# A transformer block on one core: loads held behind the modulation weights, gb folded into w_down, and a recut tail

## The chip, the cores and the metric

The kernel runs on one core of a Trainium2 chip. A core has five engines that run their own instruction streams and meet at semaphores: PE multiplies matrices, ACT applies functions, DVE does element-wise work, POOL a little of the same, and SP issues transfers (ACT can issue them too). The metric is the device time of one execution in microseconds. The time before is 896.17 us, the median of 3 runs (896.01 to 898.0). The changed kernel's time is compared with it.

## The reference

One block of a diffusion transformer: 2048 tokens, width 512, 32 heads of 16, and a gated FFN of width 1792, all bf16. A vector c gives six vectors of modulation.

```python
mod = (silu(c) @ w_mod).reshape(1, 6, 1, -1)         # w_mod 512 x 3072
sa, ca, ga, sb, cb, gb = ...                         # the six rows
h = layernorm(x) * (1 + ca) + sa
x = x + ga * attention(h)                            # 32 heads, then @ wo
h = layernorm(x) * (1 + cb) + sb
x = x + gb * ((gelu(h @ w_gate) * (h @ w_up)) @ w_down)
```

## The kernel before, in words

The kernel is written as a recorder. Each call (`mm`, `act`, `ts`, `tt`, `dma`) records one instruction for one engine, finds out which earlier instructions it must wait for from the bytes it touches, and adds the waits. Each engine then runs its list in the order in which it was recorded. So the order in the Python is the order on the engine, and a wait at one instruction holds everything behind it on that engine. SP's list is the queue of nearly all transfers.

There are three stages.

*The prologue* (`prologue`) is written out by hand. It loads c, the first four tiles of x (128 tokens each), the first third of `w_mod` (sa and ca, 1 MB) and the first 128 columns of Wq, Wk and Wv, then the rest of x, of Wqkv and of `w_mod`. PE runs filler matmuls (`warm_up`) meanwhile. silu(c) is computed by a Tanh; `mod_cols` turns it into eight columns of modulation; `ln_stat`, `ln_rstd` and `ln_norm` normalize the tiles; PE transposes them and `modulate` writes the first 512 tokens of `hT`, channels by tokens, in four channel blocks. K and Q of the first eight heads follow. `ln_rstd` runs on POOL: an addition of epsilon and a power of -0.5.

*The stream* (`stream`) is ordered by a planner that keeps its own clock of every engine while it records. Its backbone is the attention: for a group of 128 keys by 512 queries PE makes scores (`qk`), ACT takes the exponential of two or three such groups at a time (one 128 x 1024 or 128 x 1536 instruction over two or three PSUM banks), and PE multiplies by V (`pv_mms`). The planner gives some groups to DVE instead (`exp_load`, `exp_vec`: a polynomial in seven instructions over two groups). Everything else is side work in one ordered list (`plan`): the other projections, the modulation vectors, Wo, layer norm 2 and the FFN of one set of tokens after another; it is fitted in where PE has room, and its DVE steps are tasks (`task`, `step`). `SETS` cuts the queries into seven sets of 512, 512, 256, 256, 256, 128 and 128. A unit is one set with four heads (`qd` 0 to 7). `QS` says for how many `qd` the last two sets share a unit. The softmax sums go through DRAM (`pv_done`) for all units but the last ones, which use a matmul with `self32` (`near_end`, `tail_den`). The FFN inside the stream makes gelu from ACT's Tanh and DVE multiplications; `down_fin` multiplies the result by gb, adds x and stores the tile.

*The tail* (`tail`) runs when the last scores are recorded. The last set (`kb`) still needs its last sums, Wo, layer norm 2 and the whole FFN; the set before it (`ka`) has had `EARLY` chunks of its FFN's four in the stream and finishes here. `tail_end` and `tail_ffn` are generators from which the loop takes the matmul that it thinks ready first. Here gelu is an ACT function, whose table is loaded once.

In the profile nearly all instructions have the line of a helper: L308 is `mm`, L312 `transpose`, L321 `act`, L325 `tt`, L333 `ts`, L338 `stt`, L342 `copy`, L345 `recip`, L349 `memset`, L361 and L364 the statistics, L371 `dma`, L565 and L566 `ln_rstd`. They are told apart by tile: `ps_sc` is the six score banks, `ps_pv` and `ps_mi` one bank each, `E` the exponentials, `dreg` holds w_down (and, early, the normalized rows and the fillers' zeros), `mreg` w_mod and later w_gate and w_up, `wreg` Wqkv and later the FFN's input and gelu, `hreg` hT and later the FFN's product, `dt` and `dx` DVE's exponentials.

Of the kernel before, what the change touches and what calls it, by code (L numbers as in the profile page):

```python
# [14 lines left out]
P = 128  # L15
# [22 lines left out]
QS = 5  # L38
# [9 lines left out]
EARLY = 2  # L48
# [3 lines left out]
SOON = 100  # L52
END = (0, None)
# [26 lines left out]
class _Recorder:  # L80
# [285 lines left out]
    def dma(self, eng, out, in_, sem, noncontig=False, late=0):  # L366
        def fn(e):
            if noncontig:
                with self.nc.allow_non_contiguous_dma(reason="small strided transfer"):
                    return e.dma_start(out, in_)  # L370
            return e.dma_start(out, in_)  # L371
        n = mybir.dt.size(out.dtype)
        for _, k in out.ap:
            n *= int(k)
        op = self.rec(eng, fn, [in_], [out], dma=sem, cost=n)
        if op is not None:
            op.t1 += late
        return op
# [37 lines left out]
class _Kernel(_Recorder):  # L416
# [12 lines left out]
    def alloc(self):  # L429
# [32 lines left out]
        self.xw = hreg[:, NFC * 512:NFC * 512 + D]  # L462
# [7 lines left out]
        self.crow = dreg[:, 9 * D:10 * D]  # L470
        self.tcol = sb("tcol", [P, NDC], FP32)
# [17 lines left out]
    def prologue(self):  # L489
# [18 lines left out]
        self.memset(dve, self.warm, 0.0)  # L508
        self.memset(dve, self.ones[:, :], 1.0)
# [14 lines left out]
        for dc in range(NDC):  # L524
            self.mm(self.scp[:, 0, dc:dc + 1], self.crow[0:1, P * dc:P * dc + P], self.ones[0:1, 0:1])
        self.warm_up(16)
        self.act(self.tcol[:, :], self.scp[:, 0, 0:NDC], ACT.Tanh, scale=0.5)
# [3 lines left out]
        self.stt(self.tcol[:, :], self.tcol[:, :], 1.0, self.scp[:, 0, 0:NDC], ALU.add, ALU.mult)  # L531
        self.ts(dve, self.sc_bf[:, :], self.tcol[:, :], 0.5, None, ALU.mult)
# [29 lines left out]
    def ln_rstd(self, a, b):  # L562
        r = self.rstd[:, a:b]
        v, h = self.mv[:, a:b, 1], self.half[:, 0:b - a]
        self.rec("pool", lambda e: e.tensor_scalar(r, v, EPS, None, op0=ALU.add), [v], [r], cost=self.cost("pool", r, [v], "small"))  # L565
        self.rec("pool", lambda e: e.tensor_tensor(r, r, h, ALU.pow), [r, h], [r], cost=self.cost("pool", r, [r], "pow"))  # L566
# [18 lines left out]
    def mod_cols(self, bank, base):  # L585
        for ci in range(8):
            for dc in range(NDC):
                self.mm(bank[:, ci:ci + 1], self.wmod[:, dc, base + P * ci:base + P * ci + P],
                        self.sc_bf[:, dc:dc + 1], start=(dc == 0), stop=(dc == NDC - 1))
# [151 lines left out]
    def weight_parts(self):  # L741
# [11 lines left out]
        parts.append(part(self.wd[:, 12:NFC, :], v[:, 12:NFC, :], "wd12"))  # L753
# [8 lines left out]
    def scale_wo(self):  # L762
# [4 lines left out]
        yield from self.until("wo")  # L767

# [57 lines left out]
    def side_ffn(self, gi, part=None):  # L826
# [61 lines left out]
        if part is not None:  # L888
# [3 lines left out]
            return  # L892
        for i in range(n):
# [53 lines left out]
    def plan(self, ends, nsplit):  # L947
# [12 lines left out]
        w.append((lambda: self.side_q_all(2), at(133), at(160)))  # L960
        w.append((lambda: self.side_q_all(3), at(160), a + 40))
# [59 lines left out]
    def stream(self):  # L1021
# [72 lines left out]
        while pos < nseq:  # L1094
# [19 lines left out]
            if tq is not None and tq <= t + 30:  # L1114
# [9 lines left out]
                if (('v', 3, 0) in self.have and len(active) < NACT and sum(v >= 4 * rp for v in vec) < NED - (pend is None)  # L1124
                        and self.backlog() < BACK and self.free["dve"] < t + 700
                        and len(mem) == CH and slack > -100 and self.credit < (2600 if pos < ends[-3] else 1600)):
# [203 lines left out]
    def tail(self, ka, kb, half, rest):  # L1330
# [3 lines left out]
        gens += [self.tail_end(kb, f, l), self.tail_ffn(ka, self.pv[:, :], l, 0, ("part", ka))]  # L1334
        nxt = [None] * len(gens)
        table = False
        while True:
# [7 lines left out]
            best = None  # L1345
            for i, g in enumerate(gens):
# [6 lines left out]
                elif nxt[i] is not None:  # L1353
                    x = self.probe(nxt[i])
                    if best is None or max(x, t + 30) < best[0]:
                        best = max(x, t + 30), i
            w = self.next_side()
            if w is not None:
                x = self.probe(w[4][1])
# [132 lines left out]
```

## Time and profile before

| | |
|---|---|
| median of 3 runs | 896.17 us (896.01 to 898.0) |
| the profiled execution | 895.93 us, its span 894.2 us |
| ACT busy | 865.8 us, 97% of the span; of it 841.7 in exponentials |
| DVE busy | 816.4 us, 91% |
| PE busy | 811.3 us, 91% (a modelled figure) |
| granted TensorE clock | 1.00 throughout |
| modulation weights landed | 8.58 us |
| first exponential starts | 14.57 us |
| end of the last exponential | 872.55 us |
| PE's last matmul ends | 890.8 us |

A row of the timeline or of the chain gives start and length in us; a row of the groups gives the line, engine, operation, output and inputs with their shapes, the count, then busy time in us and the mean of one in ns, then the idle time of the engine ahead of it and who ended it.

### The profile page before, as it was taken

To read this page: it belongs to the slowest core of one execution; us is meant where nothing else is said; L and a number is where in the kernel's file an instruction comes from. 1 tells how busy PE (TensorE), PEld (TensorE's weight loads), DVE (VectorE), ACT (ScalarE), POOL (GpSimd) and SP (SyncE) were. 2 spreads that over 40 slices of the span, in tenths; PEclk is the share of its full clock that TensorE was granted. 3 is DMA by queue.
4 is the path that set the end of the run, shared out by engine and by line. 5 is a ranking of instruction groups with operands and counts; after the bars stand their busy time and mean duration, and the time that the engine had idled before them with its cause. 6 is when DMAs were issued, how large, how long until landed. Compare 5 with 4: busy or idle time off the path is not lost.

```text
span 894.2 us, 19936 instructions
## 1 busy us (share of the span) xinstructions
PE 811.3 (91%) x8661; PEld 286.7 (32%) x8661; DVE 816.4 (91%) x1500; ACT 865.8 (97%) x736; POOL 19.2 (2%) x36
## 2 busy tenths in 40 slices
PE   8899999988898898989999898999999999998998
PEld 3333222222222222222233222333333343334455
DVE  7778999999998999999998999998999999979955
ACT  4999999999999999999999999999999999999992
POOL 2100000000000000000000000000000000000000
PEclk9999999999999999999999999999999999999999
DMA  9012122000200000000000000010000000000100
GB/s 305 2 25 70 41 78 60 25 14 14 55 14 8 7 13 14 14 8 19 19 26 14 9 14 9 14 31 19 10 14 21 14 14 8 27 14 9 27 9 12
DMA packets 32509, 25.10 MB, mean 28 GB/s; under 512 B 16233, under 2 KB 28262, under 8 KB 32422
## 3 DMA queue, kind: packets, MB, share of 16 engines
q1 hardware_dynamic: 30566, 22.79, 8.6%
q8 instruction: 67, 1.10, 0.5%
q10 hardware_dynamic: 1856, 1.05, 0.4%
q14 instruction: 20, 0.16, 0.1%
HBM read 21.23 MB, written 2.61 MB: 27 GB/s over the span
## 4 chain that ended last, share of the span: by engine, by line
ACT 91%; PE 6%; DVE 2%; DMA 1%; issue 0%; SPq 0%
ACT E L321 88%; PE ps_sc L308 3%; ACT wreg L321 3%; PE ps_mi L308 2%; PE ps_pv L308 1%; DMA mreg<-in_w_mod_dram 1%; DVE st L361 0%; ACT hreg L321 0%; DVE dt L333 0%; DVE kmo L333 0%; DVE mreg L325 0%; DVE mreg L338 0%; SPq L371 0%; DVE hreg L325 0%; DVE wreg L338 0%
## 5 line engine op out<-in xcount | busy, mean ns | idle before, releaser
L321 ACT ACTIVATE E<-ps_sc 128x1536 bf16<-128x1536 f32 (+2 forms) x698 | 841.7, 1411 | 9.9 <-PE ps_sc L308 9.6
L308 PE MATMUL ps_sc<-qT,kme 32*128 32x256 bf16 (+2 forms) x1600 | 171.0, 304 | 13.8 <-ACT E L321 10.4
L308 PE MATMUL ps_sc<-qT,kmo 32*128 32x256 bf16 (+2 forms) x1664 | 172.2, 298 | 11.1 <-ACT E L321 7.9
L308 PE MATMUL ps_pv<-E,vaug 128*17 128x256 bf16 (+2 forms) x2884 | 179.8, 300 | 2.3 <-DVE osb L342 1.3
L333 DVE TENSOR_SCALAR dt<-ps_sc 128x512 int32<-128x512 f32 x204 | 139.0, 686 | 11.3 <-PE ps_sc L308 8.2
L308 PE MATMUL ps_sc<-kme,ident 128*128 128x512 bf16 x327 | 104.4, 384 | 36.9 <-ACT E L321 33.4
L308 PE MATMUL ps_mi<-wreg,mreg 128*128 128x256 bf16 (+2 forms) x624 | 123.6, 309 | 8.2 <-DVE wreg L342 4.0
L308 PEld LDWEIGHTS ps_sc<-qT,kmo 32*128 32x128 bf16 x1664 | 50.3, 92 | 120.2 <-ACT E L321 72.3
L308 PEld LDWEIGHTS ps_sc<-qT,kme 32*128 32x128 bf16 x1600 | 48.6, 92 | 125.2 <-ACT E L321 74.7
L308 PEld LDWEIGHTS ps_pv<-E,vaug 128*17 128x17 bf16 x2884 | 53.5, 88 | 96.8 <-issue 83.8
L325 DVE TENSOR_TENSOR qT<-qT,dx 128x1024 f16<-128x1024 f16 (+1 forms) x106 | 70.3, 664 | 1.3
L333 DVE TENSOR_SCALAR dx<-dt 128x1024 f16<-128x1024 uint16 (+1 forms) x107 | 70.0, 654 | 0.1
L308 PEld LDWEIGHTS ps_mi<-wreg,mreg 128*128 128x128 bf16 x624 | 47.7, 97 | 63.1 <-issue 30.1
L308 PE MATMUL ps_mi<-dreg,hreg 128*128 128x512 bf16 x210 | 65.3, 385 | 1.5 <-DVE wreg L338 0.8
L338 DVE SCALAR_TENSOR_TENSOR qT<-dt,qT 128x1024 int16<-128x1024 int32 (+1 forms) x53 | 62.3, 1176 | 0.1
L308 PEld LDWEIGHTS ps_sc<-kme,ident 128*128 128x128 bf16 x327 | 23.4, 97 | 88.1 <-ACT E L321 83.4
L325 DVE TENSOR_TENSOR ed<-ed,dx 128x1024 f16<-128x1024 f16 (+1 forms) x72 | 47.7, 662 | 0.7
L342 DVE CAST wreg<-ps_mi 128x512 bf16<-128x512 f32 x51 | 35.0, 686 | 11.3 <-PE ps_mi L308 10.8
L338 DVE SCALAR_TENSOR_TENSOR ed<-dt,ed 128x1024 int16<-128x1024 int32 (+1 forms) x36 | 42.2, 1172 | 0.2
L308 PE MATMUL ps_mi<-hreg,wreg 128*128 128x512 bf16 x120 | 38.7, 385 | 0.8 <-DVE vaug L342 0.5
L338 DVE SCALAR_TENSOR_TENSOR wreg<-wreg,ps_mi 128x512 bf16<-128x512 bf16 x51 | 34.7, 680 | 2.4 <-ACT wreg L321 1.8
L308 PE MATMUL ps_pv<-qT,vaug 128*17 128x256 bf16 (+2 forms) x178 | 36.5, 290 | 0.0
(126 smaller groups left out, 712.9 us busy)
## 6 DMA issues: line engine op xcount, KB each, us to landing
rb<-scr_rec SPq DMA_DIRECT2D x16, 256.0 KB
rb<-scr_rec SPq DMA_DIRECT2D x29, 128.0 KB
mreg<-in_w_mod_dram SPq DMA_DIRECT2D x1, 2048.0 KB, 12.9
out_dram<-xs SPq DMA_DIRECT2D x16, 128.0 KB, 1.7
mreg<-in_B_w_gate_dram SPq DMA_DIRECT2D x4, 448.0 KB, 7.2
mreg<-in_B_w_up_dram SPq DMA_DIRECT2D x4, 448.0 KB, 6.7
dreg<-in_B_w_down_dram SPq DMA_DIRECT2D x3, 512.0 KB, 7.6
wreg<-in_A_wqkv_dram SPq DMA_DIRECT2D x3, 384.0 KB, 9.8
```

What stands on the lines that cost most here:

```text
L308: return self.rec("pe", lambda e: e.matmul(out, lhsT, rhs, start=start, stop=stop, tile_position=tp), [lhsT, rhs], [out], cost=(n, int(rhs ...
L321: return self.rec("act", lambda e: e.activation(out, in_, func, scale=scale, **kw), rd, wr, cost=self.cost("act", out, [in_], "act" if bia ...
L325: return self.rec(eng, lambda e: e.tensor_tensor(out, a, b, op), [a, b], [out], cost=self.cost(eng, out, [a, b], "tt"))
L333: return self.rec(eng, lambda e: e.tensor_scalar(out, a, s1, s2, **kw), rd, [out], cost=self.cost(eng, out, [a], "ts" if len(rd) == 1 else ...
L338: return self.rec("dve", lambda e: e.scalar_tensor_tensor(out, a, s, b, op0=op0, op1=op1), rd, [out], cost=self.cost("dve", out, [a, b], " ...
L342: return self.rec(eng, lambda e: e.tensor_copy(out, in_), [in_], [out], cost=self.cost(eng, out, [in_], "ts"))
```

## The change

The prologue: ACT issues the first part of `w_mod` as its second transfer. The first columns of Wk, Wq and Wv are issued by SP with a dependence on that part (`after`), so SP waits for it, and all of SP's later transfers stand behind: the rest of x, which ACT's queue issued in part before, the rest of Wqkv and of `w_mod`. silu's factor of one half is folded into the matmuls that turn c (a column of 0.5 in place of ones), which saves a DVE instruction; the 1 + scale is added by PE (four matmuls of the identity with ones); two of sixteen fillers go. The modulation vector is copied by ACT. The transposes run tile by tile and not block by block, the last block's last two tiles into a bank of their own, so that ACT and DVE each take half of that block. K and Q matmuls alternate over the four blocks, into two banks.

The rest: `w_down` is multiplied by gb once, in seven DVE instructions (`scale_wd`, in the stream, when it has been loaded), and `down_fin` only adds. `QS` goes from 5 to 4 and `EARLY` from 2 to 3. In the tail, layer norm 2 of the last tile adds epsilon on DVE and normalizes the bf16 copy; its four transposes go to two banks in turn; the down projection of `ka` is a generator of its own (`tail_early`); that of the last tile has x added by PE into two half-width sums, which ACT and DVE copy and both queues store. In `tail` and `stream` a few conditions of choice change.

```diff
-QS = 5
+QS = 4
-EARLY = 2
+EARLY = 3
+FIRST = 120
@@ prologue
+        self.dma(act, self.xs[:, 0:2, :], xv[:, 0:2, :], "x0")
         self.dma(sp, self.crow[0:1, :], self.c, "c")
-        self.dma(act, self.xs[:, 0:2, :], xv[:, 0:2, :], "x0")
         self.dma(sp, self.xs[:, 2:4, :], xv[:, 2:4, :], "x1")
-        self.dma(sp, self.wmod[:, :, 0:1024], wmv[:, :, 0:1024], "wm0")
-        for k in range(3):
-            self.dma(sp if k == 1 else act, wq4[:, :, k, 0:P], wqv[:, :, k, 0:P], "wq%d" % k)
-        self.dma(sp, self.xs[:, 4:8, :], xv[:, 4:8, :], "x2")
-        self.dma(sp, self.xs[:, 8:12, :], xv[:, 8:12, :], "x3")
-        self.dma(act, self.xs[:, 12:16, :], xv[:, 12:16, :], "x4")
+        self.dma(act, self.wmod[:, :, 0:1024], wmv[:, :, 0:1024], "wm0")
+        for k in (1, 0, 2):
+            self.dma(sp, wq4[:, :, k, 0:P], wqv[:, :, k, 0:P], "wq%d" % k, after=[self.wmod[:, 0, 0:1]])
+        for i in range(2, 5):
+            self.dma(sp, self.xs[:, 4 * i - 4:4 * i, :], xv[:, 4 * i - 4:4 * i, :], "x%d" % i)
...
-        self.warm_up(16)
-        self.act(self.tcol[:, :], self.scp[:, 0, 0:NDC], ACT.Tanh, scale=0.5)
+        self.warm_up(14)
+        self.act(self.tcol[:, :], self.scp[:, 0, 0:NDC], ACT.Tanh)
...
-        self.mod_cols(self.scp[:, 1, 0:8], 0)
+        self.mod_cols(self.scp[:, 1, 0:8], 0, True)
         self.warm_up(2)
+        self.act(self.modA[:, :], self.scp[:, 1, 0:8], ACT.Copy)
         for t in range(4):
             self.ln_norm(t, self.tb1[:, 0, t, :])
-        self.copy(dve, self.modA[:, :], self.scp[:, 1, 0:8])
-        self.ts(dve, self.modA[:, 4:8], self.modA[:, 4:8], 1.0, None, ALU.add)
-        for dc in range(NDC):
-            pt = self.scp[:, 5 - dc, :].bitcast(BF16)[:, 0:512]
-            for t in range(4):
-                self.transpose(pt[:, P * t:P * t + P], self.tb1[:, 0, t, P * dc:P * dc + P], self.ident[:, :])
-            self.modulate(dve if dc % 2 == 0 else act, self.hT[:, dc, 0:512], pt, self.modA, dc)
-        bank = self.scp[:, 5, :]
-        self.proj(bank, 512, 0)
-        self.act(self.km[0][:, 0, 0:512], bank, ACT.Copy, scale=self.rm[:, 0:1])
-        self.proj_q(0, 0, self.scp[:, 4, :], dve)
-        self.ts(dve, self.km[1][:, 0, 0:512], bank, self.rm[:, 1:2], None, ALU.mult)
+        pt = [self.scp[:, 5 - dc, :].bitcast(BF16)[:, 0:512] for dc in range(NDC)]
+        px = self.scp[:, 0, :].bitcast(BF16)[:, 0:512]
+        for t in range(4):
+            for dc in range(NDC):
+                dst = px if dc == NDC - 1 and t >= 2 else pt[dc]
+                self.transpose(dst[:, P * t:P * t + P], self.tb1[:, 0, t, P * dc:P * dc + P], self.ident[:, :])
+        for eng, dc, src, a, b in ((dve, 0, pt[0], 0, 512), (act, 1, pt[1], 0, 512), (dve, 2, pt[2], 0, 512),
+                                   (act, 3, pt[3], 0, 256), (dve, 3, px, 256, 512)):
+            self.modulate(eng, self.hT[:, dc, a:b], src[:, a:b], self.modA, dc)
+        kb, qb = self.mi[:, :], self.scp[:, 1, :]
+        for dci in range(NDC):
+            for bank, col in ((kb, 512), (qb, 0)):
+                self.mm(bank, self.wqkv[:, dci, col:col + P], self.hT[:, dci, 0:512], start=(dci == 0), stop=(dci == NDC - 1))
+        self.act(self.km[0][:, 0, 0:512], kb, ACT.Copy, scale=self.rm[:, 0:1])
+        self.ts(dve, self.qT[:, 0, 0:512], qb, Q_SCALE, None, ALU.mult)
+        self.ts(dve, self.km[1][:, 0, 0:512], kb, self.rm[:, 1:2], None, ALU.mult)
@@ stream and plan
+    def scale_wd(self):
+        yield from self.until("wd")
+        if not self.dry:
+            self.task([lambda f=f: self.tt("dve", self.wd[:, f:f + 2, :], self.wd[:, f:f + 2, :],
+                                           self.gb[:, :].rearrange("p (o n) -> p o n", o=1).broadcast_to([P, 2, D]), ALU.mult)
+                       for f in range(0, NFC, 2)], "wds")
...
+        w.append((self.scale_wd, at(160), at(160)))
         w.append((lambda: self.side_q_all(3), at(160), a + 40))
...
-            self.tt("dve", self.xs[:, t, :], self.xs[:, t, :], self.xw[:, :], ALU.add)
+            self.tt("dve", self.xs[:, t, :], self.xs[:, t, :], bank, ALU.add)
...
-        return [lambda: self.tt("dve", self.xw[:, :], bank, self.gb[:, :], ALU.mult), add]
+        return [add]
@@ tail_end
-        self.task(self.ln2_steps(k, bank), ("ln2", k), self.after([("s2e", k)]), first=True)
+        v = self.mv[:, tile:tile + 1, 1]
+        steps = self.ln2_steps(k)
+        steps[0] = ("pool", lambda: self.ln_pow(tile, tile + 1))
+        self.task([lambda: self.ts("dve", v, v, EPS, None, ALU.add)] + steps, ("ln2", k), self.after([("s2e", k)]), first=True)
...
+        down = [self.mi[:, 0:D // 2], l[0][:, 0:D // 2]]
+        for i in range(2):
+            yield lambda i=i: self.mm(down[i], self.ident[:, :], self.xs[:, tile, D // 2 * i:D // 2 * i + D // 2], start=True, stop=False)
+        yield from self.tail_ffn(k, down, f, 4, None)
@@ tail_ffn
+        def fin(eng, i, queue, sem):
+            cols = slice(D // 2 * i, D // 2 * i + D // 2)
+            dst = self.xs[:, tile, cols]
+            if eng == "act":
+                self.act(dst, down[i], ACT.Copy)
+            else:
+                self.copy(eng, dst, down[i])
+            if self.probing is None:
+                self.dma(queue, self.out[0, P * tile:P * tile + P, cols], dst, sem)
+        self.task([lambda: fin("dve", 0, "sp", "out3")], None, first=True)
+        self.task([("act", lambda: fin("act", 1, "act", "out2"))], None, first=True)
```

More of the change, by code (lines that the diff above doesn't have):

```diff
@@ L364, in bn_aggr, with dma @@
         return self.rec("dve", lambda e: e.bn_aggr(out, in_), [in_], [out], cost=90)
-    def dma(self, eng, out, in_, sem, noncontig=False, late=0):
+    def dma(self, eng, out, in_, sem, noncontig=False, late=0, after=()):
         def fn(e):
@@ L374, in dma @@
             n *= int(k)
-        op = self.rec(eng, fn, [in_], [out], dma=sem, cost=n)
+        op = self.rec(eng, fn, [in_] + list(after), [out], dma=sem, cost=n)
         if op is not None:
@@ L470, in alloc @@
         self.crow = dreg[:, 9 * D:10 * D]
+        self.hbf = dreg[:, 10 * D:10 * D + 1]
         self.tcol = sb("tcol", [P, NDC], FP32)
@@ L892, in side_ffn @@
             return
+        yield from self.until("wds")
         for i in range(n):
@@ L1345, in tail @@
             best = None
+            ahead = FIRST if ("g", kb, 0) not in self.have else -FIRST
             for i, g in enumerate(gens):
@@ L1424, in up, with downs @@
             return bk
+        def downs(fcs):
+            if not lead:
+                for fc in fcs:
+                    yield lambda fc=fc: self.down_mm(down, c0 // P, fc)
+                return
+            order = [(i, fc) for fc in fcs for i in range(2)]
+            if fcs[-1] == NFC - 1:
+                order.sort()
+            for i, fc in order:
+                yield lambda i=i, fc=fc: self.mm(down[i], self.prodT[:, fc, c0:c0 + P], self.wd[:, fc, D // 2 * i:D // 2 * i + D // 2],
+                                                 start=False, stop=(fc == NFC - 1))
         if key is not None:
@@ L1427, in tail_ffn @@
         first = 0 if lead else EARLY
-        for ci in range(first):
-            for fc in chunks[ci]:
-                yield lambda fc=fc: self.down_mm(down, c0 // P, fc)
         for ci in range(first, len(chunks) + 1):
```

74 lines of the change are left out of this document (47 added, 27 removed).

## The prediction

> **What bounds the kernel now.** I read the busy time in three stretches first (columns: stretch, length, then for PE, PEld, DVE, ACT and POOL busy us and count, granted clock, DMA share, GB/s), then who waited for whom on ACT inside the middle one.
>
> ```profile
> span 894.2 us, 19936 instructions
> ```
> ```profile
> 0.00:14.57 14.57, 12.09 (x90) 5.36 (x91) 8.90 (x26) 3.59 (x6) 5.36 (x15) 1.00 0.93 286
> 14.57:872.55 857.98, 781.23 (x8357) 268.59 (x8356) 797.03 (x1455) 856.30 (x720) 13.03 (x19) 1.00 0.08 24
> 872.55:892.00 19.45, 17.93 (x217) 12.78 (x215) 10.48 (x21) 5.94 (x11) 0.80 (x2) 1.00 0.02 8
> ```
> ```profile
> ACT E L321 <- PE ps_sc L308: 1.4, 5, 0.4
> ```
>
> From the first exponential (14.57) to the end of the last (872.55) ACT is busy 856.30 of 857.98 us: the stream is ACT's own work, with 1.68 us of idle in all, 1.4 of it waits for scores. So time can come from three places only: when the first exponential starts, what ACT has to do in the stream (and whether it starts to idle), and the 19.45 us behind the last exponential with the 2.2 us of the last store. The change touches all three. The chain of work that ended last, in order of time, shows what sets the first:
>
> ```profile
> 1.66 6.92 DMA mreg<-in_w_mod_dram
> ...
> 8.71 0.94 PE ps_sc L308 x32
> 9.65 0.45 PE ps_mi L308 x2
> 10.11 0.46 PE ps_sc L312 x8
> ...
> 10.59 1.46 ACT hreg L321 x2
> ...
> 12.09 1.27 PE ps_sc L308 x5
> ...
> 13.38 0.69 DVE qT L333
> ```
>
> The reader sees one line of dependences: modulation weights land at 8.58, their matmuls, two fillers, transposes, ACT's two modulations, the last K and all four Q matmuls, Q's copy out, then the first scores and the first exponential at 14.57.
>
> **The change, part 1: the prologue.** These rows of the timeline carry it:
>
> ```profile
> 4.53 3.85 PE L308 MATMUL ps_mi<-dreg 128*128 128x512 bf16 x16
> ...
> 8.44 0.73 DVE L333 TENSOR_SCALAR dreg<-xs,mv,rstd 128x512 bf16<-128x512 bf16 x2 [0.61 <-POOL rstd L566]
> ...
> 9.94 1.05 PE L312 MATMUL ps_sc<-ident,dreg 128*128 128x128 bf16 x16
> 10.37 0.99 DVE L333 TENSOR_SCALAR hreg<-ps_sc,modA 128x512 bf16<-128x512 bf16 x2 [0.31 <-PE ps_sc L312]
> ...
> 14.57 3.71 ACT L321 ACTIVATE E<-ps_sc 128x1536 bf16<-128x1536 f32 x3 [1.36 <-PE ps_sc L308]
> ...
> 14.65 0.68 DVE L361 BATCH_NORM_STATS2 st<-xs 128x6 f32<-128x512 bf16 x1
> ```
>
> And the transfers: all loads of 2.00 to 8.60 together ran at the rate that ends the first row; below it are landing times (KB each, median us to landing).
>
> ```profile
> 2.00:8.60 6.60, 6.38 (x26) 2.34 (x24) 4.88 (x16) 1.46 (x2) 4.32 (x6) 1.00 1.06 323
> ```
> ```profile
> wreg<-in_A_wqkv_dram SPq DMA_DIRECT2D x1, 128.0 KB, 8.2
> xs<-in_A_x_dram ACTq DMA_DIRECT2D x1, 256.0 KB, 2.8
> ```
>
> *Landing of the modulation weights.* Before, 2.1 MB moved by 8.6 (323 GB/s over 6.6 us); the two loads of x that must come first and the weights themselves are 1.57 MB. With the rest held back, the same rate from 2.0 gives 2.0 + 1.57/0.323 = 6.9. The load moves to ACT's queue as its second issue; ACT has nothing else to do then.
>
> *PE ahead of the modulation.* Sixteen fillers took 3.85, 0.24 each, to 8.38; fourteen end at 7.9, behind the landing at 6.9. So PE, no longer the load, sets the start of the modulation matmuls: 7.9 instead of 8.71, 0.8 earlier. Four matmuls against the identity are added there (the 1 + scale), at 0.94/32 = 0.03: 0.12. The fillers' 0.45 stays. Transposes start at 9.25 instead of 9.94 (the chain counts them from 10.11, the end of the fillers). The normalized rows they read were ready at 8.44 + 0.73 = 9.17, and one DVE instruction ahead of them goes: no wait. The DVE copy and add that made the modulation vector become one ACT copy beside PE: nothing.
>
> *Modulation.* Transposes now run tile by tile, so the first channel block is complete only at the 13th of 16, at 0.46/8 = 0.058 each: 9.25 + 0.75 + about 0.15 = 10.15, only 0.2 ahead of 10.37. But ACT's share falls from two blocks (1.46) to one and a half (0.73 + 0.45), DVE's rises from 0.99 to 0.99 + 0.4: DVE ends last, near 11.55, where ACT ended at 12.05. Gain 0.5.
>
> *K and Q.* Before, one K and four Q matmuls followed the last block (1.27); now one K and one Q, some 0.6. Gain 0.67. ACT's and DVE's copies behind them run side by side as before. First exponential: 14.57 - 0.5 - 0.6 = **13.45, a gain of 1.1**.
>
> *What the held loads cost.* SP now waits for the modulation weights, and behind that wait stand in order K's, Q's and V's weights, three loads of x, the rest of the weights and the second modulation load. K's weights are issued at about 6.95, Q's at 7.45. If they land as the first load of x did (2.8), Q's are there at 10.25, before the first K matmul near 10.75: hidden by 0.5. If they take what the contended load took (8.2), Q's land at 15.65. I take 2.8, since the queues are empty then. [...] Tiles 4 to 7 of x come next; their first use on DVE was at 14.65, some 2 us behind their landing by the same rate.
>
> **Part 2: the stream.** The order written by the planner changes in count, and counts can be compared between the two programs: exponentials over three banks 460 to 457, over two banks 232 to 235 (three more score groups go to DVE), and one more Tanh over 512. By form, and from the chain:
>
> ```profile
> L321 ACT ACTIVATE E<-ps_sc 128x1536 bf16<-128x1536 f32 x460 | 651.8, 1555 | 2.8 <-PE ps_sc L308 2.5
> L321 ACT ACTIVATE E<-ps_sc 128x1024 bf16<-128x1024 f32 x232 | 245.3, 1150 | 0.2 <-PE ps_sc L308 0.2
> ```
> ```profile
> 671.81 0.51 ACT wreg L321
> ```
>
> Three times 1.555 - 1.150 is 1.2 off, the Tanh 0.5 on: **0.7 gained**, if ACT idles no more than before. DVE pays: 16 multiplications by gb from PSUM go, 7 over w_down of the kind below (0.684) come, and the three groups and an FFN chunk. With DVE at 797.03 of 857.98 there is room on average.
>
> ```profile
> L325 DVE TENSOR_TENSOR ed<-ed,dx 128x1024 f16<-128x1024 f16 x66 | 45.1, 684 | 0.6
> ```
> ```profile
> 160.90 0.48 SPq L371 DMA_DIRECT2D dreg<-in_B_w_down_dram x1
> ...
> 180.72 0.52 SPq L371 DMA_DIRECT2D scr_den<-osb  x1
> ```
>
> The seven wait for w_down, whose last part is issued at 160.9; they stand about the seventh copy-out of an attention unit, which the last row puts near 180. They do not wait. The Q projections of the last tokens are queued behind them as side work and are not due until the sets near the end of the sequence. The split of sets 5 and 6 into separate units one unit earlier changes no exponential's size.
>
> **Part 3: the tail.**
>
> ```profile
> 876.00 0.22 PE ps_sc L308
> ...
> 879.11 0.93 PE ps_pv L308 x4
> ...
> 881.50 3.58 PE ps_sc L308 x61
> ...
> 889.48 1.31 PE ps_mi L308 x6
> ...
> 890.82 0.70 DVE hreg L325
> ...
> 891.54 0.42 DVE xs L325
> ```
> ```profile
> 877.56 0.58 POOL L566 TENSOR_TENSOR rstd<-rstd,half 128x1 f32<-128x1 f32 x1
> 878.25 0.69 DVE L338 SCALAR_TENSOR_TENSOR hreg<-ps_sc,E 128x512 bf16<-128x512 f32 x1 [1.09 <-PE ps_sc L308]
> 878.86 0.80 DVE L333 TENSOR_SCALAR dx<-ps_sc,mv,rstd 128x512 bf16<-128x512 f32 x1
> 880.18 0.81 ACT L321 ACTIVATE wreg<-ps_sc,modB 128x128 bf16<-128x128 bf16 x2 [1.10 <-PE ps_sc L312]
> 880.75 0.69 DVE L333 TENSOR_SCALAR wreg<-ps_sc,modB 128x128 bf16<-128x128 bf16 x2 [0.76 <-PE ps_pv L308]
> ```
>
> *To the last tile's FFN.* rstd is ready at 878.14, but DVE first does a 0.69 product of the other tile, then a 0.80 normalization from PSUM. A third FFN chunk of that tile now lies in the stream, so this product is gone from here (a small one stands ahead of the statistics, where DVE idles), and the normalization reads bf16 from SBUF (0.40 by the last fence's first row). It ends at 878.6 instead of 879.66. Eleven down matmuls of the other tile stand ahead of its transposes on PE: from 876.2, behind the last W_o matmul, at 1.31/6 = 0.22 each, to 878.6, just in time (today four more, the row of 879.11, hold the transposes to 880.0). The four modulations now alternate between two banks, so ACT and DVE run side by side: ACT 878.9 to 879.7. The free run of up matmuls starts at 879.75 instead of 881.50. Gain 1.75. The epsilon on DVE in place of POOL: nothing either way.
>
> *To the end.* From 881.50 to 890.79 PE never waits, and its columns stay the same; 28 half-width down matmuls for 14 cost between nothing and 0.02 each, 0.5 in all; I take 0.1, as PE is paced by columns in these rows. Two identity matmuls hide beside the modulations. Behind PE, 0.70 + 0.42 become one half-tile copy from PSUM (0.38 by the fence's second row), on ACT and DVE at once: 0.74 gained. The store is half as large per queue; I leave its 2.2.
>
> ```profile
> L333 DVE TENSOR_SCALAR dreg<-xs,mv,rstd 128x512 bf16<-128x512 bf16 x16 | 5.6, 404 | 1.2 <-POOL rstd L566 1.2
> ...
> L321 ACT ACTIVATE E<-ps_sc 128x256 bf16<-128x256 f32 x2 | 0.8, 384 | 2.2 <-PE ps_sc L308 2.2
> ```
>
> **Tail gain 2.4.** Sum: 1.1 + 0.7 + 2.4 = 4.2 of 895.93, the profiled execution's time (span 894.2 and 1.73 around it), gives 891.7; the median 896.17 stands 0.24 above that execution, so I forecast **892.0**.
>
> **Rivals.**
> *The held loads come late.* Q's weights land after 10.75. Each 1 us more costs 1 us. For: a 128 KB load took 8.2 among others. Against: 2.8 where little was in flight. If all of the prologue's gain goes, 893.1; at 8.2, Q lands 4.9 late: 896.9.
> *ACT starts to idle in the stream.* For: the planner places work by its own costs, the seven products of w_down come in runs of up to three beside score conversions, 2.1 us against one exponential in hand (1.4), so up to 0.7 a run, and DVE is short of room locally. Against: 1.68 idle in 858 us today. With 2 to 4 us of new idle, 894 to 896.
> *The other side: DVE becomes the bound.* The same conversions run late throughout, so that PE's score banks are not freed and ACT waits. It decides where new ACT idle exceeds the 4.2 gained; slower by over 0.3% needs 7. Free DVE time today is 61 us and some 8 are added, so this needs the free time to lie in the wrong places: 899 to 901.
> *The tail's gain does not come.* An earlier normalization meets PE still in the other tile's down matmuls or the attention's last unit waits for its reciprocal through DRAM, now taken later on DVE: 894.1.
>
> **How the numbers follow.** Chances: forecast 0.62 (own range 890.5 to 893.2); late loads 0.12; idle 0.16; DVE bound 0.05; tail 0.05. A measurement here tells 0.3%, 2.7 us, from no change: faster ends at 893.5, slower starts at 898.9. Faster takes the forecast and half of late loads and part of idle, 0.74; slower the DVE case and a little of the late loads, 0.06; same 0.20. The range reaches from 890.2 (today's idle gone as well) to 895.8, inside the idle case.
>
> **What would show it.** First exponential near 13.45, modulation matmuls at 7.9 right behind the fillers; if they start later, the load was late, and if K's first matmul waits for a DMA, the held loads were. ACT idle from first to last exponential about 1.7. From last exponential to PE's last matmul 16.5 instead of 18.2, then one copy. The prediction is wrong if ACT's idle is several us, or if the Q weights end a wait.

## The result, and the profile after

The changed kernel takes **893.96 us** (median of 7 runs, 893.75 to 895.08) against 896.27 (median of 7, 896.01 to 898.22) for the kernel before on the same chip. The ratio is 0.9968, with a 95% interval of 0.9958 to 0.9978: faster by 0.32%, 2.3 us of the 4.2 that the sum had.

The profiled execution took 893.76 us. Its busy time in the same three stretches (columns as before: length, PE, PEld, DVE, ACT, POOL busy us and count, granted clock, DMA share, GB/s), cut at the first and the last exponential of the changed kernel:

```profile
0.00:13.55 13.55, 10.98 (x90) 5.33 (x92) 8.71 (x25) 3.56 (x6) 5.35 (x15) 1.00 0.69 220
13.55:873.11 859.56, 758.27 (x8390) 275.04 (x8518) 806.22 (x1478) 855.75 (x721) 12.78 (x19) 1.00 0.09 25
873.11:890.20 17.09, 16.22 (x200) 12.32 (x199) 8.52 (x19) 5.83 (x11) 0.56 (x1) 1.00 0.03 10
```

The reader sees where the time went. "Tail" is from the end of the last exponential to the end of the span (892.0 here, 894.2 before):

| us | before | after | difference | forecast |
|---|---|---|---|---|
| start of the first exponential | 14.57 | 13.55 | -1.02 | -1.1 |
| stream: ACT busy | 856.30 | 855.75 | -0.55 | -0.7 |
| stream: ACT idle | 1.68 | 3.81 | **+2.13** | 0 |
| tail | 21.65 | 18.89 | -2.76 | -2.4 |
| span | 894.2 | 892.0 | -2.2 | -4.2 |

Three of the four terms came about as forecast. ACT's work fell by the counted instructions (groups of the same forms as in the prediction):

```profile
L322 ACT ACTIVATE E<-ps_sc 128x1536 bf16<-128x1536 f32 x457 | 648.7, 1556 | 4.3 <-PE ps_sc L309 3.9
L322 ACT ACTIVATE E<-ps_sc 128x1024 bf16<-128x1024 f32 x235 | 248.1, 1146 | 0.2 <-PE ps_sc L309 0.2
```

What was lost is 2.13 us of new ACT idle in the stream. The timeline of ACT shows it in ten places; here are the two longest, and the rows of DVE and PE that stand ahead of the first of them (start, length, engine, operation, count, and in brackets the idle before with its releaser):

```profile
23.33 0.39 PE L313 MATMUL ps_mi<-ident,dreg 128*128 128x128 bf16 x4
...
23.97 0.40 PE L313 MATMUL ps_mi<-ident,dreg 128*128 128x128 bf16 x4
...
26.22 1.04 PE L309 MATMUL ps_mi<-hreg,wreg 128*128 128x512 bf16 x4
...
27.30 0.75 DVE L334 TENSOR_SCALAR kme<-ps_mi,rm 128x512 bf16<-128x512 f32 x1 [0.44 <-PE ps_mi L309]
...
28.11 0.38 PE L309 MATMUL ps_sc<-qT,kme 32*128 32x512 bf16 x1 [0.53 <-DVE kme L334]
...
28.53 2.37 ACT L322 ACTIVATE E<-ps_sc 128x1536 bf16<-128x1536 f32 x2 [0.96 <-PE ps_sc L309]
...
603.62 1.45 ACT L322 ACTIVATE E<-ps_sc 128x1536 bf16<-128x1536 f32 x1 [0.56 <-PE ps_sc L309]
```

The first is a short line of dependences: the K projection of the second 512 tokens runs at 26.22, DVE copies K out at 27.30, the next scores need it at 28.11, and ACT has run dry by 0.96. Before, the same rows were:

```profile
24.06 0.62 PE L312 MATMUL ps_mi<-ident,dreg 128*128 128x128 bf16 x8
...
26.01 1.04 PE L308 MATMUL ps_mi<-hreg,wreg 128*128 128x512 bf16 x4
...
27.09 0.75 DVE L333 TENSOR_SCALAR kme<-ps_mi,rm 128x512 bf16<-128x512 f32 x1
```

K came 0.2 later than before although ACT, and all that uses K, had started 1.0 earlier. The planner has changed the order: the second eight of that block's sixteen transposes are split into two fours, and the K matmuls stand behind 30 score matmuls on PE where they stood behind 28.

### The profile page after: what moved, and what is told of

Its sections match the earlier page's. It is cut to its first block, busy times and chain, and to the rows that moved or that the text cites. A ratio compares the mean times of both kernels' runs of the same rounds, so it can differ in the third digit from the quotient of the medians.

```text
span 892.0 us, 20136 instructions
## 1 busy us (share of the span) xinstructions
PE 785.5 (88%) x8677; PEld 292.7 (33%) x8809; DVE 823.4 (92%) x1520; ACT 865.1 (97%) x738; POOL 18.7 (2%) x35
## 4 chain that ended last, share of the span: by engine, by line
ACT 87%; PE 10%; DVE 3%; issue 0%
ACT E L322 84%; PE ps_sc L309 4%; PE ps_mi L309 4%; ACT wreg L322 3%; PE ps_pv L309 1%; DVE dt L334 0%; DVE wreg L339 0%; DVE st L362 0%; DVE dx L334 0%; DVE kme L334 0%; DVE qT L334 0%; DVE wreg L343 0%; DVE kmo L334 0%; DVE osb L343 0%; DVE hreg L326 0%
## 5 line engine op out<-in xcount | busy, mean ns | idle before, releaser
L309 PE MATMUL ps_sc<-qT,kme 32*128 32x256 bf16 (+2 forms) x1664 | 169.2, 298 | 20.1 <-ACT E L322 15.2
L309 PE MATMUL ps_sc<-qT,kmo 32*128 32x256 bf16 (+2 forms) x1664 | 170.1, 298 | 15.2 <-ACT E L322 10.3
L334 DVE TENSOR_SCALAR dt<-ps_sc 128x512 int32<-128x512 f32 x207 | 141.0, 685 | 11.4 <-PE ps_sc L309 8.5
L309 PE MATMUL ps_sc<-kme,ident 128*128 128x512 bf16 x273 | 90.2, 384 | 46.4 <-ACT E L322 43.9
L309 PE MATMUL ps_mi<-wreg,mreg 128*128 128x256 bf16 (+2 forms) x637 | 117.7, 301 | 8.4 <-DVE wreg L339 3.5
L326 DVE TENSOR_TENSOR qT<-qT,dx 128x1024 f16<-128x1024 f16 (+1 forms) x112 | 74.0, 661 | 1.1
L309 PEld LDWEIGHTS ps_mi<-wreg,mreg 128*128 128x128 bf16 x656 | 50.3, 97 | 56.2 <-issue 26.8
L339 DVE SCALAR_TENSOR_TENSOR qT<-dt,qT 128x1024 int16<-128x1024 int32 (+1 forms) x56 | 65.4, 1169 | 0.1
L309 PE MATMUL ps_mi<-dreg,hreg 128*128 128x512 bf16 (+1 forms) x183 | 56.3, 375 | 2.7 <-issue 2.1
L309 PE MATMUL ps_pv<-qT,vaug 128*17 128x256 bf16 (+2 forms) x186 | 38.9, 291 | 0.0
```

The source lines that it names most:

```text
L309: return self.rec("pe", lambda e: e.matmul(out, lhsT, rhs, start=start, stop=stop, tile_position=tp), [lhsT, rhs], [out], cost=(n, int(rhs ...
L326: return self.rec(eng, lambda e: e.tensor_tensor(out, a, b, op), [a, b], [out], cost=self.cost(eng, out, [a, b], "tt"))
L334: return self.rec(eng, lambda e: e.tensor_scalar(out, a, s1, s2, **kw), rd, [out], cost=self.cost(eng, out, [a], "ts" if len(rd) == 1 else ...
L339: return self.rec("dve", lambda e: e.scalar_tensor_tensor(out, a, s, b, op0=op0, op1=op1), rd, [out], cost=self.cost("dve", out, [a, b], " ...
```

## The experiments

The kernel before varied from 895.5 to 898.6 us from run to run, so profiled executions are compared by stage, and times by medians with intervals.

**The prologue alone.** The kernel before with `prologue`, `mod_cols` and `dma` of the changed kernel; all else as before.

```diff
-        self.dma(sp, self.wmod[:, :, 0:1024], wmv[:, :, 0:1024], "wm0")
+        self.dma(act, self.wmod[:, :, 0:1024], wmv[:, :, 0:1024], "wm0")
+        for k in (1, 0, 2):
+            self.dma(sp, wq4[:, :, k, 0:P], wqv[:, :, k, 0:P], "wq%d" % k, after=[self.wmod[:, 0, 0:1]])
...
```

> The kernel before with the new prologue alone (loads, fillers, modulation, transposes, K and Q); stream constants, w_down and tail as before. First exponential at 13.55 as in the changed kernel. Theory (the planner, with the held Wk, Wq and Wv on its clock, puts the K matmuls of the second 512 tokens one score group later, so ACT runs out of scores near 28 us): idle of some 1.0 near 28 us gives the gain back, time 896.1, no change against before. Rival (that idle comes with the rest of the change): no idle near 28 us, time 895.2.

897.18 us, ratio 1.0007 (0.9999 to 1.0016): nothing gained. The 0.96 of idle is there (at 29.73, with the first exponential at 14.76), the stream's idle is 2.74, ACT's busy time and the tail are before's (856.48 and 21.62). So the idle belongs to the new prologue. It is as long as the 1.0 us by which the changed kernel starts earlier; that it eats just this microsecond is not shown here, since this execution's first exponential came no earlier than the 14.57 of before (its fillers took 4.41 us, see the table of starts).

**All but the prologue.** The changed kernel with the prologue of the kernel before.

```diff
-        self.dma(act, self.wmod[:, :, 0:1024], wmv[:, :, 0:1024], "wm0")
-        for k in (1, 0, 2):
-            self.dma(sp, wq4[:, :, k, 0:P], wqv[:, :, k, 0:P], "wq%d" % k, after=[self.wmod[:, 0, 0:1]])
...
+        self.dma(sp, self.wmod[:, :, 0:1024], wmv[:, :, 0:1024], "wm0")
+        for k in range(3):
+            self.dma(sp if k == 1 else act, wq4[:, :, k, 0:P], wqv[:, :, k, 0:P], "wq%d" % k)
...
```

> The changed kernel with the old prologue. First exponential at 14.57, tail 2.75 shorter than before. Theory: no idle near 28 us; the stream has only the scattered idle, some 2.6 to 2.8 in all, so the time is 896.3 - 2.75 - 0.55 + 1.1 = 894.1, as the whole change. Rival (the scattered idle belongs to the prologue): stream as before less 0.55, time 893.0.

895.41 us, ratio 0.9983 (0.9971 to 0.9996). No idle near 28 us, ACT busy 855.95, tail 18.90. The expected 894.1 was missed: the profiled execution started late (first exponential 17.37), and 1.14 us of ACT idle stands at 508 to 512 us, of which more below. Its other idle stands at the changed kernel's places and has the same lengths (0.55 at 608, 0.29 at 846 the longest), so the prologue does not make that idle.

**No hold.** The changed kernel without the dependence on the modulation weights. It was run twice; both expectations stand here.

```diff
-            self.dma(sp, wq4[:, :, k, 0:P], wqv[:, :, k, 0:P], "wq%d" % k, after=[self.wmod[:, 0, 0:1]])
+            self.dma(sp, wq4[:, :, k, 0:P], wqv[:, :, k, 0:P], "wq%d" % k)
```

> The changed kernel, Wk, Wq and Wv not held behind the modulation weights, same order on SP's queue. The planner's order of the K matmuls is that of before. Theory (holding pays in the transfer, costs in the order): modulation weights near 8.6, first exponential near 14.4, no idle near 28 us, time 893.9, as with the hold. Rival (the hold brings nothing to the landing): first exponential 13.6, time 893.0. Rival (late data, not the order): idle near 28 us stays, 894.8.

> The changed kernel without the hold, a second profiled execution. By the account that the hold makes the landing of the modulation weights early enough in every execution (7.4 to 8.9 us in six held ones) and its absence leaves it to chance: modulation matmuls at 8.7 to 10.5 us again, behind a wait for a DMA. By the rival that the first execution was the exception: 7.6 to 8.2 us right behind the fillers. [...]

893.67 us, ratio 0.9964 (0.9951 to 0.9977), and 892.74, ratio 0.9965 (0.9952 to 0.9978), the second below the 893.5 to 895 expected. The K matmuls stand behind 28 score matmuls again, and no idle is at 28 us in either. The starts differ by 3 us between two executions of one program: modulation matmuls at 9.77 behind a wait for the load, and at 7.96 right behind the fillers. So the account in the second expectation (modulation matmuls at 8.7 to 10.5, behind a wait) held in the first execution, and its rival (7.6 to 8.2) in the second; the first exponential of 14.4 in the first expectation came in neither.

**The hold, with another planner's clock.** The changed kernel, in which only the planner's estimate of when the held loads land is 1 us earlier. The transfers and the prologue's instructions are those of the changed kernel; PE's order becomes that of the kernel without the hold. Also run twice.

```diff
-..., "wq%d" % k, after=[self.wmod[:, 0, 0:1]])
+..., "wq%d" % k, after=[self.wmod[:, 0, 0:1]], late=-1000)
```

> The changed kernel, loads held as in it; only the planner's clock is told that Wk, Wq and Wv land 1 us earlier than it thinks, which gives the K matmuls of the second 512 tokens the place they had before. Theory (order): first exponential 13.55, no idle near 28 us, time 893.0, 1.0 below the changed kernel. Rival (the held data come late in fact): idle near 28 us stays, time 894.0.

> The changed kernel with the other planner's clock once more. Its first execution had no idle near 28 us but lost 1.09 us at 507 us, where the granted clock was 0.55 to 0.60 behind two pauses of PE; the changed kernel has the same pauses at 502 to 504 us and kept the clock at 1.00 in both executions. If the dip is chance, this execution has none and its stream idle is 2.8 us (3.94 less 1.09), with a span near 891 if the fillers are short (3.19) and 892.5 if they are long (4.32); if it is a consequence of the order, it stands there again, idle 3.9 us. Median 893.0 to 893.9.

893.84 us, ratio 0.9971 (0.9961 to 0.9981), and 894.07, ratio 0.9969 (0.9958 to 0.9979). The idle at 28 us is gone in both: ACT's row of the second one runs from 18.70 over 122 exponentials without a gap above 0.06 us.

```profile
18.70 141.71 ACT L322 ACTIVATE E<-ps_sc 128x1024 bf16<-128x1024 f32 x122 [0.25 <-PE ps_sc L309]
```

The stream's idle in the second was 2.77, which is the changed kernel's 3.81 less 0.96 and a little. This settles the first half of the new idle: the held loads are not late themselves, the *planner's picture of them* moves the K projection behind two more score matmuls. Yet the median did not fall by 0.96. Part of the reason stands in the first one's windows of granted clock, and in those of the kernel without the hold, which has the same order there:

```profile
503.00:505.00 2.00, 1.07 (x9) 0.25 (x9) 2.00 (x4) 2.00 (x3) 0.00 (x0) 1.00 0.00 0
505.00:507.00 2.00, 2.00 (x17) 0.36 (x16) 1.99 (x4) 1.92 (x2) 0.00 (x0) 0.55 0.04 8
507.00:509.00 2.00, 2.00 (x18) 0.42 (x17) 0.43 (x1) 1.40 (x2) 0.00 (x0) 0.60 0.00 0
```

```profile
503.47 0.41 PE L309 MATMUL ps_sc<-kme,ident 128*128 128x512 bf16 x1 [0.93 <-ACT E L322]
...
506.51 1.45 ACT L322 ACTIVATE E<-ps_sc 128x1536 bf16<-128x1536 f32 x1 [0.60 <-PE ps_sc L309]
508.37 10.00 ACT L322 ACTIVATE E<-ps_sc 128x1536 bf16<-128x1536 f32 x8 [0.40 <-PE ps_sc L309]
```

The first fence is the first execution with the other clock, the second the second execution without the hold. Behind a PE pause of 0.93 us (one of 0.21 stands 1.9 us ahead of it) the granted clock falls to 0.55 for about 4 us, PE is then too slow for ACT, and ACT idles 1.0 to 1.1 us more. The other execution of each program has the same matmuls there and a pause of 0.92 or 0.93, and keeps the clock at 1.00. Of the five profiled executions with K behind 28 score matmuls in this stream (the rest alone is the fifth) three had the dip; of the changed kernel's two, which have pauses of 0.92 and 0.93 there, none, nor of its two variants below.

The granted clocks of all runs say more. The mean over the execution was 1.00 in all 12 runs of the changed kernel, and 0.998, as in the profiled execution with the dip, in 8 of the 17 runs with the other clock. Those 8 took 894.3 to 895.8 us, the other 9 took 892.5 to 893.8. So between these two programs the loss of clock goes with the order, and with the other order it comes in about half of the runs: a good part of what that order saves is lost again. This is no rule for the K order in other streams: the prologue alone, with K behind 30 score matmuls, shows 0.998 or 0.999 in 7 of its 11 runs. Where the clock fell in the runs without a profile is not known, the sets ran on different chips, and why the same pauses cost the clock in one order and not in the other is open.

**The changed kernel once more.**

> The changed kernel once more, for a second profiled execution of the same program. If the order of the program makes the ACT idle of 0.96 us at 28.5 us and the scattered 1.2 us beyond before's, both stand at the same places again: idle in the stream about 3.8 us, the wait behind DVE's copy of the second K near 28 us plus whatever the first exponential has moved, tail 18.9 us, busy time of ACT in the stream 855.7 us. If they are chance, idle is 1.7 to 2.7 us and lies elsewhere. The start is expected not to repeat: the 14 fillers of the first execution took 3.19 us while the same 14 took 4.32 us in the version with the other planner's order, so the first exponential may come anywhere between 13.5 and 15.3 us with nothing changed; if it comes at 13.55 again, the program sets it. Time 893 to 895 us.

893.86 us, ratio 0.9968 (0.9956 to 0.9981). The stream's idle was 3.80, at the same ten places to 0.01 us each (the two longest again 0.96, at 28.32, and 0.55), tail 18.91. The start was 13.35.

**The set before the last with two chunks in the stream.**

```diff
-EARLY = 3
+EARLY = 2
```

> The changed kernel with EARLY back at 2: the set before the last has two and not three of its FFN chunks in the stream. My account of the tail says that the third chunk's product (0.69 us on DVE) then again stands ahead of the last tile's normalization: the free run of up matmuls starts 0.5 to 0.7 us later, and the tail is 19.4 to 19.6 us instead of 18.88. Against it stands one Tanh over 512 columns less on ACT in the stream (0.5 us), so the time is that of the changed kernel within 0.3 us. The rival, that the gain comes from the recut alone (transposes in two banks, half-tile copies, normalization from SBUF): tail 18.9 us, and 0.5 us faster than the changed kernel.

895.09 us, ratio 0.9979 (0.9971 to 0.9988): 1.23 slower than the changed kernel beside it. Both expectations missed: the tail is 20.46, 1.55 longer, and the stream's work 0.5 shorter. The timeline, then the chain that ended last (start, length, engine, tile, count):

```profile
877.46 0.69 DVE L339 SCALAR_TENSOR_TENSOR hreg<-ps_sc,E 128x512 bf16<-128x512 f32 x1
877.62 0.56 POOL L576 TENSOR_TENSOR rstd<-mv,half 128x1 f32<-128x1 f32 x1 [22.83 <-DVE mv L334]
...
878.29 0.41 DVE L334 TENSOR_SCALAR dx<-xs,mv,rstd 128x512 bf16<-128x512 bf16 x1
...
878.77 0.39 PE L313 MATMUL ps_sc<-ident,dx 128*128 128x128 bf16 x4
```

```profile
880.15 0.92 PE ps_sc L309 x16
881.07 0.22 PE ps_pv L309
881.29 0.06 PE ps_sc L309
881.34 1.29 PE ps_pv L309 x6
882.64 2.51 PE ps_sc L309 x45
```

DVE's product of the other tile is back, but it runs while POOL takes the power, so the transposes come at 878.77, no later than the changed kernel's 878.83. What costs is PE: the third chunk's up and down matmuls (`ps_pv`, six together here) stand in the middle of the last tile's FFN, and PE is never idle there. The stream's idle stands at the changed kernel's places with the same lengths, so the third chunk does not make it.

**The folding of gb alone.** The kernel before with `scale_wd`, its place in the plan, the two marks that order it (w_down loaded, w_down scaled), and the single addition in `down_fin`.

```diff
-        return [lambda: self.tt("dve", self.xw[:, :], bank, self.gb[:, :], ALU.mult), add]
+        return [add]
...
+        w.append((self.scale_wd, at(160), at(160)))
```

> The kernel before with only the folding of gb into w_down: seven multiplications of w_down in the stream, and one addition from PSUM per tile in place of a multiplication and an addition. ACT gets 462 and 230 exponentials over three and two banks instead of 460 and 232, which is 0.8 us more work. If the folding makes the new scattered idle, ACT idles 2.7 to 3.0 us in the stream instead of 1.69; if not, about 1.7. The tail ends 0.4 us earlier (0.70 and 0.42 become one of 0.68), 21.2 us. By the first, 897.2 us; by the second, 896.4 us (the kernel before: 896.3).

899.61 us, ratio 1.0029 (1.0017 to 1.0040): slower, and by more than either expectation. ACT busy 857.33 and idle 2.67 in the stream, 1.03 and 0.98 more than before; tail 21.42. That makes 1.8 of the 2.7; this execution also started late (first exponential at 16.38). The idle is not near the seven products, which run from 204 to 212 us. The longest new one, 0.97, stands at 576; the chain ahead of it:

```profile
573.58 0.60 DVE qT L325
574.18 0.34 DVE ed L333
574.52 1.14 DVE qT L338
575.66 0.04 issue
575.71 0.39 PE ps_pv L308 x5
576.09 0.35 PE ps_sc L308 x6
576.44 0.02 issue
576.47 1.45 ACT E L321
```

PE's multiplication by V waits for an exponential that DVE is still making, and the scores that ACT needs stand behind it on PE.

**Without the new condition on DVE's share.**

```diff
-(self.credit < (2600 if pos < ends[-3] else 1600) or (pos >= ends[0] and self.next_side() is None))
+self.credit < (2600 if pos < ends[-3] else 1600)
```

> The changed kernel without the new condition under which the planner gives score groups to DVE when no side work is left: 464 and 228 exponentials over three and two banks instead of 457 and 235, so seven groups more on ACT, 7 x 0.405 = 2.8 us more busy time (858.5 in the stream). If these extra groups on DVE cause the scattered idle (DVE's conversions late, score banks not freed), the idle falls from 3.8 to about 2.7 us and the kernel is 1.7 us slower than the changed one; if the idle has nothing to do with them, it stays at 3.8 and the kernel is 2.8 us slower, 896.7 us.

897.57 us, ratio 1.0009 (1.0000 to 1.0018), 3.7 slower than the changed kernel beside it. ACT's busy time is 3.1 more, and the idle rises a little, to 4.21, where one theory wanted 2.7. So the extra groups on DVE do not raise the total. They do decide where it falls: without them the changed kernel's idle between 375 and 723 us (0.56 at 603 the longest) is gone, and 0.37 at 315, 0.97 at 575 and 0.19 at 612 stand in its place, as with the folding alone (0.37 at 317, 0.97 at 576, 0.19 at 613):

```profile
574.74 36.75 ACT L322 ACTIVATE E<-ps_sc 128x1536 bf16<-128x1536 f32 x31 [0.96 <-PE ps_sc L309]
```

The new condition is what makes the rest of the change pay: with the folding but without it, ACT has 464 exponentials over three banks.

**The kernel before once more.**

> The kernel before once more, for a second profiled execution. The four executions so far in which nothing is held (before, the rest alone, no hold, the fold alone) had the modulation matmuls at 8.71, 10.46, 9.77 and 9.45 us, each time ended by the landing of the weights, and first exponentials at 14.57 to 17.37. If the landing varies from execution to execution, this one has its modulation matmuls anywhere between 8.7 and 10.5 us and the time moves with it, 895.9 to 898; if before's profile was typical, 8.7 and 895.9. The stream repeats in either case: ACT busy 856.30, idle 1.7 us, tail 21.6 us.

897.12 us in the profiled execution. Stream and tail repeat (busy 856.32, idle 1.70, tail 21.63); the start does not:

```profile
9.90 0.94 PE L308 MATMUL ps_sc<-sc_bf,mreg 128*128 128x1 bf16 x32 [0.91 <-DMA mreg<-in_w_mod_dram]
```

The first exponential came at 15.75. Put together, the thirteen profiled executions say this of the start:

| program | issue to landing of the first modulation load | PE's wait for it | fillers took | first exponential |
|---|---|---|---|---|
| not held, 16 fillers: before, twice | 6.9, 8.1 | 0.33, 0.91 | 3.85, 4.46 | 14.57, 15.75 |
| not held, 16: fold alone, rest alone | 7.6, 8.7 | 1.26, 1.93 | 3.65, 4.01 | 16.38, 17.37 |
| not held, 14: no hold, twice | 8.4, 6.4 | 2.05, none | 3.19, 3.59 | 17.02, 13.94 |
| held, 14: prologue alone | 5.8 | none | 4.41 | 14.76 |
| held, 14: the changed kernel, twice | 5.8, 5.8 | none | 3.19, 3.19 | 13.55, 13.35 |
| held, 14: two chunks, no condition | 5.9, 6.0 | none | 3.65, 3.19 | 14.01, 13.50 |
| held, 14: other clock, twice | 7.5, 5.9 | none | 4.32, 4.39 | 15.26, 14.75 |

The hold does what it was said to do: PE never waited for the load. What is left of the spread, 1.9 us between the first and the last of the seven held ones, is mainly the length of the same 14 fillers, 3.19 to 4.41: the first exponential follows their end by 5.82 or 5.83 us in six of them, and by 6.41 in the one whose load took 7.5. By their medians the kernels with and without the hold cannot be told apart (0.9964 and 0.9965 against 0.9968 to 0.9971), but their runs spread differently. Without the hold 6 of the 11 runs took 892.65 to 892.95 us, less than any of the changed kernel's 12 (893.54 to 895.08), and the other five, with a mean clock of 0.998, took 894.4 to 896.2. The hold removes the wait for the load, and the order that comes with it costs the best times.

## Why the prediction was right, and where it was not

The time, 893.96, lies inside the range of 890.2 to 895.8 and on the side forecast; the forecast of 892.0 was 2 us too low, mainly for one reason. The range was wide enough to hold the case of new idle in the stream, and by the time alone the prediction was right; of the mechanism, part 2 failed, and parts 1 and 3 came near their totals by other steps than those named, which is luck.

*The step that failed* is in part 2: "**0.7 gained**, if ACT idles no more than before". The work went down by 0.55; the idle went up by 2.13. It was written down as a rival (894 to 896), given 0.16, and this is, by its size, the case that came. But the mechanism named there, runs of w_down's products beside score conversions, is not what happened: ACT has no new idle by them. Two others did. The hold, part of the prologue, changes the planner's clock and with it the order of the second K projection: 0.96, shown by its presence with the prologue alone and its absence in both executions with the other clock. The other 1.17 is scattered (0.56 at 603, 0.29 at 841, the rest near 0.2). The prologue and the third chunk are excluded, since this idle repeats without them. The folding alone brings 0.98, but at other places, and without the new condition on DVE's share the idle moves to those places. So where it falls belongs to the order that the planner writes; that any new order costs about 1 us here is a guess, and which part of the change costs it stays open (`QS` was not tried alone). The prediction compared the two programs by *count* of ACT's instructions; it did not compare their *order* on PE at the places where ACT has one exponential in hand, though the planner fixes that order before any run.

*Prologue: 1.02 of 1.1, by other parts than named.* The modulation matmuls came at 7.56, right behind the fillers as said, 0.3 better than 7.9: the 14 fillers took 3.19 and not 3.4, and the first of these matmuls starts 0.16 before the end of the last filler. DVE's last modulation ended at 11.13 and not at 11.55. But "Gain 0.67" for K and Q did not come:

```profile
10.43 0.39 PE ps_mi L309
10.81 0.22 PE ps_sc L309
...
12.11 0.23 PE ps_sc L309
12.34 0.02 issue
12.36 0.69 DVE qT L334
```

The eight alternating matmuls run one after another from 10.43 at 0.22 each, so PE and no longer the last block sets their end: 1.21 behind the last modulation, where it was 1.31. The gain is 0.10. (The prediction worked out 0.67 and added only 0.6; with 0.67 its first exponential would be 13.40.) The three differences, 0.92 to the end of the modulation, 0.10 for K and Q, and nothing behind, make the 1.02.

*Held loads.* In the profiled execution of the changed kernel Q's weights were there in time (KB each, median us from issue to landing):

```profile
mreg<-in_w_mod_dram ACTq DMA_DIRECT2D x1, 1024.0 KB, 5.8
wreg<-in_A_wqkv_dram SPq DMA_DIRECT2D x3, 128.0 KB, 2.7
```

The 2.7 stands beside the 2.8 that was taken. The margin was real and thin: in the one held execution whose modulation load took 7.5 us, PE waited 0.20 for Q's weights. As the cause of the missing gain the rival of late loads falls, since PE waits for no DMA behind the fillers in the changed kernel's two executions.

*Tail: 2.76 where 2.4 was said, and again for another reason.* From the last exponential to the free run of up matmuls it took 8.95 before and 6.96 now, 1.99 less where 1.75 was said; from there to PE's end 0.10 more, as taken (a half-width down matmul took 0.11, a full one before 0.22; that a half-width one could cost up to 0.02 more was an estimate); the half-tile copies gave 0.77 for 0.74; the store 0.10.

```profile
878.84 0.34 PE ps_sc L313 x3
879.18 0.02 issue
879.21 0.82 ACT wreg L322 x2
880.02 0.05 issue
880.07 3.64 PE ps_sc L309 x62
...
889.48 0.38 ACT xs L322
```

The account put the gain on DVE: the 0.69 product "gone from here" and the cheaper normalization, with PE's down matmuls of the other tile "just in time". With `EARLY` at 2 the product is back and costs nothing, while the tail is 1.55 longer through PE's work. More than half of the tail's gain is thus the third chunk's matmuls, moved from a tail in which PE is the bound to a stream in which ACT is. The price there was counted rightly: a Tanh, 0.5.

*The median.* The forecast set 896.17 beside a profiled 895.93 and took the difference as noise around one start. A second execution of the kernel before started 1.2 us later with nothing changed. The single profile used for the sum was one of the kernel's good starts.

## What to carry to other kernels

When a change lets a planner write a new order, count the instructions but also lay the two orders side by side at each point where the bounding engine has only one piece of work in hand; a load that is held back on the chip also moves the planner's clock. Work moved from a stage bound by one engine to a stage bound by another can pay (here 1.55 us off PE's tail for 0.5 on ACT's stream), so ask for each stage which engine is never idle there, and not only which step stands last in the chain. A stage that begins with a transfer, and with matmuls whose length differs from one execution to the next (14 fillers took 3.19 to 4.41 us here), needs several profiled executions before its time is used in a sum.

## What the runs showed of the hardware

In these executions the granted clock fell after pauses of PE between 0.93 and 2.05 us, and not after each of them. Without the hold, a PE wait of 2.05 us for the modulation weights (it ended at 9.77) was followed by half clock from 12 to 14 us; the mean over the longer stretch that contains the wait reads 0.79 (columns as in the table of stretches):

```profile
8.00:16.00 8.00, 5.71 (x62) 3.48 (x62) 2.21 (x6) 1.79 (x4) 0.13 (x1) 0.79 1.10 333
12.00:14.00 2.00, 1.68 (x11) 0.86 (x10) 1.31 (x3) 1.23 (x2) 0.00 (x0) 0.50 1.09 334
```

The same 0.79 stands behind waits of 1.26 and 1.93, and 1.00 behind 0.33 and 0.91. In the stream a pause of 0.93 without the hold was followed by 0.50 in one execution (505 to 507 us) and by 1.00 in the other. The 14 fillers took 3.19 to 4.41 us (single fillers 0.38 to 0.63), though the column of the granted clock reads 1.00 there. What decides whether the clock falls behind such a pause, and what makes the fillers longer, these runs do not show.
